# A recurrent-attention and mixer kernel on one core: plain up products in batches 1 and 2, casting loads for k of batch 0, and a new order of all steps

## Chip, core and metric

The kernel runs on one core of a Trainium2 chip. A core has TensorE (PE, the matmuls), VectorE (DVE), ScalarE (ACT), GpSimd (POOL) and SyncE (SP, which here only issues DMAs). POOL issues DMAs too, and only those can change the type of the data on their way. The metric is the device time of one launch in microseconds. Before the change the median of three runs is 233.54 us (233.43 to 233.62).

## What is computed

```python
B, H, S, D = 4, 8, 768, 64            # batches, heads, positions, head width; d_model = H*D = 512
state = gamma[h]*state + k_t v_t^T    # per batch and head, over the positions t
y_t   = q_t^T state / sqrt(D)
x     = y with the heads side by side                      # (4, 768, 512)
u     = x + ((x^T U) V)^T                                  # U 768x32, V 32x768
out   = u + relu(u @ w_ch1) @ w_ch2                        # 512x2048 and 2048x512
```

The inputs and the output are float32; the products run in bfloat16.

## The kernel before

The recurrence is computed in chunks: inside a chunk as masked scores, between chunks through a state of 64 by 64 per head. q, k and v are scaled by powers of gamma on the way, and the 1/sqrt(D) goes into q.

Every step of the kernel is one word of a list, `ORDER`. The word gives the step, its batch and block, the engine (E for PE, D for DVE, A for ACT, P for POOL, S for SP) and the PSUM banks that it opens. Each engine runs its steps in the order of the list, one behind the other, and waits at a step whose input is not there yet. The 8 banks of PSUM are handed out in the list as well: a step that opens a bank waits until the last reader of its former content is done. A second list, `LOADS`, gives the first loads in SP's queue.

The steps that matter here:

- **Head (batch 0).** `load_q6` (L274) and `load_early` (L284, L293) load q, k and v as float32. `ck` casts k to bf16 (`cast_early`, L440), `cv` scales v, `cq` scales q (L387), all in a layout with two neighbouring positions per partition. `tk`, `tq` turn k and q on PE (L458, L407), `ek`, `eq` copy the turned tiles from PSUM. `sc` are the scores (L474), `ma` the masking (L481), `st`, `cs` the states (L912) and their copies, `mx`, `qy`, `ox` the mixing (L502, L890, L902) and its copy into x. `pr`, `pc`, `xt`, `ex`, `uT` make u (L941 to L960). `fi` are filler matmuls on zeros (L932). `lu` and `lv` load U and, four times, V by casting loads from POOL (L346, L349).
- **Weights.** `w1a` to `w1e` and `w2.j` are casting loads from POOL (L352, L357). `gate` (L381) is a one-row copy on POOL that reads w2's third quarter and writes into the tile that q of batch 1 will use; so it holds POOL's queue until that quarter has landed, and the loads of q until then.
- **Attention of batches 1 to 3, in six chunks.** `lq`, `lk`, `lv` load a chunk (L376), `pk` casts k, `pq` and `pv` scale q and v (`prep`, L518). On ACT a scaling is eight instructions, one for each head (L527); on POOL or DVE it is one (L256). `dk`, `dq` turn k and q by a DMA transpose from SP (L554); batch 1 turns on PE. Then `sc` (L564), `ma` (L571), `st` (L582), `cs`, `mx` (L599, L604), `ox` as above.
- **u of batches 1 to 3.** `pj` (L623), `pc`, `xp` (L635), `xa` (L641) add the low-rank part; `du` turns x by DMA transposes (L647), in batch 1 PE does it (L654).
- **Up product, batch 0.** `U.b.m.h` (L721) is 4 matmuls of 384 columns into one bank: column block m of 16, half h of the positions. `V.b.m.h` is the relu that empties the bank (ACT L710, DVE L712).
- **Up product, batches 1 to 3.** Seven half-size products for each of 8 pairs of column blocks, `Q1` to `Q7` (L782), two matmuls each. They need sums of u (`us`, four on DVE) and of w1 (`VS`, 4 sets, once, written into w1's own tile). Behind them stand nine steps for each pair: copies `c1`, `c5`, `c6`, `c7`, adds `x2`, `x3`, `x7`, relus `r1`, `x4`, `r2`.
- **Down product, all batches.** Seven half-size products for each of 3 pairs of position blocks, `P1` to `P7` (L829), eight matmuls of 256 columns each, with sums of g before them (`s1` to `s4`) and of w2 (`Ta`, `Tb`, once), and adds (`c`, `a`, `x`) behind them. `s0`, `s1` with a `d` are the stores (L874).

Of the kernel before, what the change touches and what calls it, by code (L numbers as in the profile page):

```python
# [9 lines left out]
fp32 = mybir.dt.float32  # L10
# [5 lines left out]
LOADS = "q0 q1 q3 q2 k01 v01 k00 v00 k11 v10 v11 k10 k20 v20 v23 k21 v21 v22".split()  # L16
ORDER = (
# [175 lines left out]
def kernel(  # L193
# [72 lines left out]

    tmpA = big.tile([P, 12288], bf16, tag="gT", name="early_a")
    tmpB = big.tile([P, 9216], bf16, tag="sg", name="early_b")


    qin = {0: qin_tile(0)}

# [876 lines left out]
```

## Time and profile before

| what | value |
|---|---|
| median of 3 runs | 233.54 us (233.43 to 233.62) |
| the profiled execution, and its span | 231.99 us, 230.2 us |
| first up matmul, batch 0 | 28.25 us |
| first up matmul of batches 1, 2, 3 | 87.71, 139.03, 186.68 us |
| first down matmul of batches 0 to 3 | 53.27, 111.43, 163.29, 207.51 us |
| last matmul ends | 226.75 us |
| mean granted TensorE clock | 0.997 |
| chain that ended last | PE 43%, DVE 23%, ACT 11%, DMA 10% |

The page gives the busy time of each engine, the chain that is followed back from the last instruction, and groups of instructions by line and shape with their busy time, count and mean duration, and the idle time ahead of them. A helper's line stands for many steps: L249 is every ACT copy, L256 every two-input step on DVE or POOL, so the tiles and shapes tell the groups apart. Matmul records overlap, because the next one starts before the last one has left the array. DVE and ACT records overlap by a little as well, so that busy time over count is nearer to the distance between two starts than the mean duration is.

### The profile page before, as it was taken

The numbers are of one execution on the slowest core, as the hardware profiler recorded it, in microseconds if no ns is written. First come the engines' busy times: TensorE is split into PE (matmuls) and PEld (weight loads), VectorE is DVE, ScalarE is ACT, GpSimd is POOL, SyncE is SP. The second block draws the span as 40 slices with busy tenths as digits, with TensorE's granted clock in tenths as the row PEclk, the third lists the DMA queues.
The fourth block names the chain that finished last, engine by engine and source line by source line (L and its number), as shares of the span: only waits on it lengthen the run. The fifth ranks groups of instructions, "written<-read, shape, count | busy, mean of one in ns | idle before, by whom it ended". The sixth has DMA issues, their size and how long they took to land.

```text
span 230.2 us, 6231 instructions
## 1 busy us (share of the span) xinstructions
PE 210.3 (91%) x2420; PEld 149.8 (65%) x2420; DVE 190.4 (83%) x412; ACT 147.4 (64%) x400; POOL 97.5 (42%) x111
## 2 busy tenths in 40 slices
PE   7989999999699699997859999989999979999993
PEld 7977656557486576554546785545687856557883
DVE  5789488499978787999999767999899559999842
ACT  2578657678389998995994605888972127873100
POOL 3169125111999461585482224374371201442120
PEclk9999999999999999999999999999999999999998
DMA  6999999999989943895279479998732561001024
GB/s 191 307 289 173 162 173 256 235 197 231 209 175 231 216 77 67 168 230 138 54 145 171 104 149 175 212 236 101 152 114 71 137 117 46 3 0 48 0 111 165
DMA packets 86558, 34.73 MB, mean 151 GB/s; under 512 B 71233, under 2 KB 84161, under 8 KB 86529
## 3 DMA queue, kind: packets, MB, share of 16 engines
q1 hardware_dynamic: 79920, 27.01, 54.1%
q0 software_dynamic: 6608, 7.33, 16.6%
q8 instruction: 19, 0.31, 0.6%
q14 instruction: 11, 0.08, 0.1%
HBM read 27.75 MB, written 6.29 MB: 148 GB/s over the span
## 4 chain that ended last, share of the span: by engine, by line
PE 43%; DVE 23%; ACT 11%; DMA 10%; SPq 6%; issue 4%; DVEq 0%; POOL 0%
PE bank L782 17%; PE bank L829 16%; DVE gT L256 6%; DVE sg L256 5%; DMA qin<-in_q_dram 4%; ACT qd L527 3%; SPq L284 3%; DMA uT<-x 3%; ACT vd L527 3%; DVE gT L712 3%; DVE w2t L256 3%; DMA k<-in_k_dram 2%; PE bank L564 2%; DVE x L641 2%; SPq L647 2%
## 5 line engine op out<-in xcount | busy, mean ns | idle before, releaser
L249 ACT ACTIVATE part<-bank 128x384 f32<-128x384 f32 x73 | 33.6, 495 | 23.0 <-PE bank L782 22.3
L829 PEld LDWEIGHTS <-gT 128*128 128x128 bf16 x384 | 36.2, 98 | 5.7 <-issue 0.4
L256 DVE TENSOR_TENSOR gT<-bank,part 128x384 bf16<-128x384 f32 x64 | 32.5, 548 | 0.7 <-PE bank L782 0.5
L829 PEld LDWEIGHTS <-sg 128*128 128x128 bf16 x288 | 26.9, 98 | 9.3 <-issue 4.3
L710 ACT ACTIVATE gT<-bank 128x384 bf16<-128x384 f32 x50 | 23.8, 493 | 8.2 <-PE bank L721 7.6
L829 PE MATMUL bank<-w2b,sg 128*128 128x256 bf16 x192 | 24.6, 273 | 1.9 <-DVE a L571 1.9
L782 PEld LDWEIGHTS <-w1b 128*128 128x128 bf16 x192 | 17.9, 98 | 12.6 <-issue 1.5
L782 PE MATMUL bank<-uT,w1s 128*128 128x384 bf16 x96 | 21.6, 326 | 3.1 <-DVE part L251 1.4
L571 DVE TENSOR_TENSOR a<-bank,mask 128x512 bf16<-128x512 f32 x36 | 23.5, 681 | 1.1 <-PE bank L564 1.1
L829 PE MATMUL bank<-w2t,gT 128*128 128x256 bf16 x192 | 23.8, 273 | 0.2 <-ACT part_d L249 0.2
L829 PE MATMUL bank<-w2b,gT 128*128 128x256 bf16 x192 | 24.0, 273 | 0.0
L721 PE MATMUL bank<-uT,w1b 128*128 128x384 bf16 x128 | 22.3, 326 | 0.6 <-DVE gT L712 0.6
L782 PEld LDWEIGHTS <-w1s 128*128 128x128 bf16 x144 | 13.3, 98 | 14.1 <-issue 4.1
L527 ACT ACTIVATE vd<-in_v,gk 128x64 bf16<-128x64 f32 x88 | 22.0, 352 | 0.0
L782 PE MATMUL bank<-uS,w1b 128*128 128x384 bf16 x96 | 21.5, 326 | 0.3 <-DVE gT L256 0.2
L782 PE MATMUL bank<-uT,w1b 128*128 128x384 bf16 x96 | 21.3, 326 | 0.3 <-DVE gT L256 0.3
L641 DVE TENSOR_TENSOR x<-bank,x 128x256 bf16<-128x256 f32 x48 | 17.2, 416 | 3.5 <-PE bank L635 3.4
L256 DVE TENSOR_TENSOR o<-bank,part_d 128x256 f32<-128x256 f32 x34 | 14.2, 420 | 6.1 <-PE bank L829 5.8
L249 ACT ACTIVATE x<-bank 128x256 bf16<-128x256 f32 (+2 forms) x39 | 13.5, 387 | 6.7 <-PE bank L604 5.1
L721 PEld LDWEIGHTS <-w1b 128*128 128x128 bf16 x128 | 12.0, 98 | 8.5 <-issue 0.9
L256 POOL TENSOR_TENSOR sg<-sg,gT 128x768 bf16<-128x768 bf16 (+1 forms) x6 | 9.2, 1528 | 18.0 <-DVE sg L256 18.0
L256 POOL TENSOR_TENSOR gT<-part,part 128x384 bf16<-128x384 f32 x7 | 7.0, 1002 | 21.6 <-ACT part L249 21.6
(130 smaller groups left out, 407.2 us busy)
## 6 DMA issues: line engine op xcount, KB each, us to landing
in_k<-in_k_dram SPq DMA_DIRECT2D x18, 256.0 KB, 4.9
in_v<-in_v_dram SPq DMA_DIRECT2D x18, 256.0 KB, 5.0
out_dram<-o SPq DMA_DIRECT2D x13, 256.0 KB, 2.2
qin<-in_q_dram SPq DMA_DIRECT2D x8, 384.0 KB, 5.6
in_q<-in_q_dram SPq DMA_DIRECT2D x12, 256.0 KB, 4.1
out_dram<-o POOLq DMA_DIRECT2D x11, 256.0 KB, 2.7
w2b<-in_moe_w_ch_dram POOLq DMA_DIRECT2D x4, 512.0 KB, 12.7
k<-in_k_dram SPq DMA_DIRECT2D x6, 256.0 KB, 5.9
```

The source lines that it names most:

```text
L249: nc.scalar.activation(dst, src, AF.Copy)
L256: (nc.vector if eng == "D" else nc.gpsimd).tensor_tensor(dst, a, b, op=op)
L284: nc.sync.dma_start(out=t, in_=src)
L527: nc.scalar.activation(t[:, h], src[:, h], AF.Copy, scale=g[:, ci, h:h + 1])
L564: nc.tensor.matmul(sb[i][:, ts(hp, P)], kqT[b, ci][r, 0, hp], qt[r, hp], start=True, stop=True)
L571: nc.vector.tensor_tensor(live["a", b, ci][:, i], score_p[b, "s", ci][i].rearrange("p (n m) -> p n m", n=NHP), mask[:, None, :].to_broadca ...
L641: nc.vector.tensor_tensor(xg, live["h", b, jp][c][:, :256].rearrange("p (j e) -> p j e", j=2), xg, op=ALU.add)
L710: nc.scalar.activation(dst, src, AF.Relu)
L712: nc.vector.tensor_relu(dst, src)
L721: nc.tensor.matmul(g_p[:, :HT], w1b[:, c, ts(m, P)], uTs[b][:, c, ds(HT * h, HT)], start=(c == 0), stop=(c == NCB - 1))
L782: nc.tensor.matmul(dst[:, :HT], lhs[:, c], rhs(c), start=(n in (1, 2, 5) and c == 0), stop=(n in (2, 3, 4) and c == 1), skip_group_check=True)
L829: nc.tensor.matmul(dst, lhs[:, i], rhs[:, i], start=(n in (1, 2, 5) and i == 0), stop=(n in (2, 3, 4) and i == NI - 1), skip_group_check=True)
```

## The change

- Batches 1 and 2 use the plain up product (`U`, `V`) in place of `Q1` to `Q7`, their posts and the sums of u. Batch 3 keeps the seven products. The sums of w1 move from the first third of the list to the end of batch 2's up product.
- k of batch 0 is loaded by six casting loads from POOL (`Lk`) straight into bf16; the six casts `ck` go. The layout is [head, position pair] now, so that `turn_k` turns one head at a time, 8 transposes in place of 4 for each `tk`.
- U and V are loaded once as float32 by SP, at the end of `LOADS`, and cast on chip: U on POOL (`cU`), V four times (`cV0` on POOL, `cV1` to `cV3` on ACT).
- `g0`, a copy of one row on POOL, waits for the first piece of v's last block, ahead of w1's first load.
- w1's columns are asked for in the order a, b, c, d, e, and w1e behind the gate; w2's third quarter goes out between w1c and w1d.
- The whole order is new, and with it the engines of many steps. The scalings of q and v leave ACT altogether.

Steps of the main part by engine, where their number changes much:

| steps | before | after |
|---|---|---|
| Q products, U products | 168, 32 | 56, 96 |
| relus V in batches 1 and 2 | none | ACT 46, DVE 18 |
| scalings pq and pv | ACT 16, POOL 14 | POOL 26, DVE 4 |
| sums of w1 (sets) | POOL 3, DVE 1 | POOL 2, DVE 2 |

```diff
-LOADS = "q0 q1 q3 q2 k01 v01 k00 v00 k11 v10 v11 k10 k20 v20 v23 k21 v21 v22".split()
+LOADS = "q1 q0 q2 q3 v01 v00 v20 v11 v10 v23 v22 v21 V U".split()
...
+    lowr = big.tile([P, 4 * S], fp32, tag="w2t", name="lowr")
+    Vf = lowr[:RK, :S]
+    Uf = lowr[:, ds(S, NCK * RK)].rearrange("p (j r) -> p j r", j=NCK)
...
-    def load_u():
-        nc.gpsimd.dma_start(out=Ub, in_=moe_U.rearrange("(j p) r -> p j r", p=P))
-
-    def load_v(c):
-        nc.gpsimd.dma_start(out=V4[ds(RK * c, RK)], in_=moe_V)
+    def cast_u(eng):
+        copy(eng, Ub, Uf)
+
+    def cast_v(c, eng):
+        copy(eng, V4[ds(RK * c, RK)], Vf)
...
-    kb = [carve(tmpA, 3072 * i, [2, H, D]) for i in range(NB)]
+    kb = [carve(tmpA, 3072 * i, [H, 2, D]) for i in range(NB)]
...
+    def load_k0(B0, f):
+        nc.gpsimd.dma_start(
+            out=kb[B0][:, ds(4 * f, 4)].rearrange("p h j d -> p h (j d)"),
+            in_=k[0, ds(4 * f, 4), ds(256 * B0, 256), :].rearrange(
+                "h (t j) d -> t h (j d)", j=2))
...
     def turn_k(B0, f):
         tps[B0, f] = bank(bf16)
-        for hp in (2 * f, 2 * f + 1):
+        for n in range(2):
             for j in range(2):
-                nc.tensor.transpose(tps[B0, f][:, ts(2 * (hp % 2) + j, P)],
-                                    kb[B0][:, j, ds(2 * hp, 2)], ident)
+                for i in range(2):
+                    nc.tensor.transpose(
+                        tps[B0, f][ds(D * i, D), ts(2 * n + j, P)],
+                        kb[B0][:, 4 * f + 2 * n + i, j], ident)
...
+        elif nm == "g0":
+            nc.gpsimd.tensor_copy(out=hold, in_=early["v", 2, 0][:1, 0, :8])
```

The new order in the places that the steps of the prediction touch, in its own words: POOL's part of the head, the start of batch 1's up product, and the place where batch 2's down product meets batch 3's up product.

```
Lk00:P cq0:P ... Lk01:P Lk21:P Lk20:P ... Lk11:P ... Lk10:P ... cv00:P ... g0:P ... cv20:P ... cv11:P ... w1a:P
... cv23:P cv22:P ... cv21:P ... cU:P ... w1b:P ... cV0:P ... w1c.0:P ... w2.2:P ... w1d.0:P ... gate.0:P ... w1e.0:P ... w2.3:P

pj.1:E:3 ... tu.1.1:E:3 xp.1.2:E:0627 ... st.2.0:E:4 ... P4.0.d2:E ... ou.1.1:A U.1.14.0:E:5 ... U.1.2.0:E:7 ... tu.1.2:E:6

P6.2.d2:E Q1.3.0:E:5 ... P4.2.d1:E ... Q5.3.0:E:1 ... P7.2.d2:E ... P3.2.d1:E ... Q1.3.1:E:7 Q6.3.0:E Q1.3.2:E:4
Q5.3.1:E:2 ... P2.2.d2:E:6 ... P4.2.d2:E ... P3.2.d2:E Q2.3.0:E:6
```

More of the change, by code (lines that the diff above doesn't have):

```diff
@@ L280, in load_early @@
     def load_early(nm, B0, f):
-        src = {"k": k, "v": v}[nm][0, ds(4 * f, 4), ds(256 * B0, 256), :].rearrange(
+        src = v[0, ds(4 * f, 4), ds(256 * B0, 256), :].rearrange(
             "h (t j) d -> t h (j d)", j=2)
@@ L295 @@
     for nm in LOADS:
-        if nm[0] == "q":
+        if nm == "U":
+            nc.sync.dma_start(out=Uf, in_=moe_U.rearrange("(j p) r -> p j r", p=P))
+        elif nm == "V":
+            nc.sync.dma_start(out=Vf, in_=moe_V)
+        elif nm[0] == "q":
             load_q6(0, int(nm[1]))
@@ L311, in ramp @@
         return t
+    hold = consts.tile([1, 8], fp32)
     zeros = consts.tile([P, 512], bf16)
@@ L440, in cast_early @@
     def cast_early(nm, B0, f, eng, h0=0, nh=4):
-        dst = {"k": kb, "v": vb}[nm][B0]
         hs = ds(4 * f + h0, nh)
-        dst = dst[:, :, hs]
         src = early[nm, B0, f][:, ds(h0, nh)].rearrange("p h (j d) -> p j h d", j=2)
-        if nm == "k":
-            copy(eng, dst, src)
-        else:
-            scale = gk2[:, B0, hs].rearrange("p h j -> p j h")
-            binary(eng, dst, src, scale[:, :, :, None].to_broadcast([P, 2, nh, D]),
-                   ALU.mult)
+        scale = gk2[:, B0, hs].rearrange("p h j -> p j h")
+        binary(eng, vb[B0][:, :, hs], src,
+               scale[:, :, :, None].to_broadcast([P, 2, nh, D]), ALU.mult)
+    def load_k0(B0, f):
[3 more added lines that the diff above has]
+                "h (t j) d -> t h (j d)", j=2))
     tps = {}
@@ L912, in state0 @@
                     nc.tensor.matmul(st_p[ds(D * i, D), ds(P * c + D * i, D)],
-                                     kb[B0][r, j, 2 * c + i], vb[B0][r, j, 2 * c + i],
+                                     kb[B0][r, 2 * c + i, j], vb[B0][r, j, 2 * c + i],
                                      start=False, stop=True, skip_group_check=True)
@@ L970, in early_step @@
             turn_q6_out(0, x[0], eng)
-        elif k2 == "ck":
-            cast_early("k", x[0], x[1], eng)
+        elif k2 == "Lk":
+            load_k0(x[0], x[1])
         elif k2 == "tk":
@@ L1013, in early_step @@
             out_uT(x[0], 0, eng)
-        elif nm == "lu":
-            load_u()
-        elif nm == "lv":
-            for c in range(NCB):
-                load_v(c)
+        elif nm == "cU":
+            cast_u(eng)
+        elif k2 == "cV":
+            cast_v(x[0], eng)
+        elif nm == "g0":
+            nc.gpsimd.tensor_copy(out=hold, in_=early["v", 2, 0][:1, 0, :8])
         elif nm in ("w1a", "w1b"):
```

329 rows, old and new, of the table ORDER are left out of this document.

## The prediction

> **What bounds the kernel now.** I read the page's busy rows first, then the stages in a table of windows, then the groups, then the chain. I cut the span at the first matmul of each up product (U) and down product (D) of batches 0 to 3. The columns are: stretch, length, then PE, PEld, DVE, ACT and POOL busy, clock, DMA share, GB/s.
>
> ```profile
> PE 210.3 (91%) x2420; PEld 149.8 (65%) x2420; DVE 190.4 (83%) x412; ACT 147.4 (64%) x400; POOL 97.5 (42%) x111
> ```
> ```profile
> 0.00:28.25 28.25, 26.37 (x516) 21.96 (x517) 19.93 (x46) 17.18 (x41) 12.87 (x26) 1.00 1.05 225
> 28.25:53.27 25.02, 23.87 (x184) 14.03 (x181) 19.88 (x44) 16.62 (x33) 7.00 (x8) 1.00 1.14 218
> 53.27:87.71 34.44, 30.01 (x439) 23.68 (x437) 28.44 (x66) 29.51 (x99) 24.95 (x22) 1.00 0.87 183
> 87.71:111.43 23.72, 22.31 (x194) 12.36 (x192) 23.09 (x45) 20.20 (x46) 12.21 (x13) 1.00 0.66 142
> 111.43:139.03 27.60, 24.24 (x315) 19.14 (x313) 23.09 (x47) 15.54 (x59) 10.46 (x11) 1.00 0.66 129
> 139.03:163.29 24.26, 22.39 (x194) 12.53 (x192) 23.14 (x47) 20.47 (x52) 11.70 (x11) 1.00 1.00 190
> 163.29:186.68 23.39, 23.39 (x315) 19.07 (x313) 18.65 (x44) 9.92 (x33) 8.48 (x11) 1.00 0.48 104
> 186.68:207.51 20.83, 19.00 (x114) 10.85 (x112) 19.69 (x42) 15.40 (x34) 6.21 (x5) 1.00 0.10 38
> 207.51:226.75 19.24, 18.68 (x170) 16.18 (x167) 14.11 (x36) 2.51 (x7) 3.65 (x5) 1.00 0.19 70
> ```
>
> The stages are the head, then U0, D0, U1, D1, U2, D2, U3, D3. In the three seven-product stages (U1, U2, U3) DVE is busy 94 to 97% of the time; in D0 ACT is busy for 29.5 of 34.4 us. PE seems as full, but its records overlap. The groups say 326 ns for a 384-column matmul, while the chain has 32 of them in a row in 5.20 us:
>
> ```profile
> 77.73 1.91 ACT qd L527 x8
> 79.80 1.91 ACT qd L527 x8
> ...
> 82.50 1.91 ACT qd L527 x8
> ...
> 97.59 5.20 PE bank L782 x32
> ```
>
> So one costs 0.163 us from start to start. In the PE timeline 24 down matmuls of 256 columns take 2.78 us, 0.109 each. Counting all PE steps of a stage at such pitches (score 0.33, state 0.245, mixing 0.48, projection 0.45, expansion 0.31 us a step) gives PE's bare work: 23.3, 28.0, 21.0, 22.8, 20.9, 22.8, 18.3, 18.3 us, together 175.4. The stages took 198.5. The difference, 23.1 us (1.7, 6.4, 2.7, 4.8, 3.4, 0.6, 2.5, 0.9), is PE waiting. Most of it lies in D0, D1 and U2. The chain runs through it on DVE and ACT, as the three scalings above show: eight small ACT instructions each, 1.91 us.
>
> The Trainium skill ("Perfetto Trace Analysis", Identifying the Most-Contended Engine) says that matmul busy time does not measure how full PE is, as matmuls are pipelined. The rows agree (326 against 163 ns). By busy time the added matmuls would cost 32 x 0.326 = 10.4 us; nothing below uses that.
>
> **Up product of batches 1 and 2.** Seven products on 8 blocks are 112 matmuls; sixteen columns by two halves by four steps are 128. PE gains 2 x 16 x 0.163 = 5.2 us. Around it much goes:
>
> ```profile
> L249 ACT ACTIVATE part<-bank 128x384 f32<-128x384 f32 x73 | 33.6, 495 | 23.0 <-PE bank L782 22.3
> L256 DVE TENSOR_TENSOR gT<-bank,part 128x384 bf16<-128x384 f32 x64 | 32.5, 548 | 0.7 <-PE bank L782 0.5
> L710 ACT ACTIVATE gT<-bank 128x384 bf16<-128x384 f32 x50 | 23.8, 493 | 8.2 <-PE bank L721 7.6
> L527 ACT ACTIVATE vd<-in_v,gk 128x64 bf16<-128x64 f32 x88 | 22.0, 352 | 0.0
> ```
>
> Busy over count: an ACT copy 0.46, a DVE add 0.51, an ACT relu 0.476. Batch 1 has 36 DVE steps of this kind (x2, x3, c7, relus, four sums of u), 18.6 us; the new order has 11 relus of 0.53, 5.9 us. On ACT 40 steps, 20.7 us, become 21, 10.0 us. Batch 2: DVE 17.8 to 3.7, ACT 20.4 to 11.9. The sums of u go with them; PE waited 0.32 us for one in batch 2 (at 141.74). With fewer posts, banks are freed sooner.
>
> **Scalings and casts.** V and q scalings on ACT (8 x 0.25 = 2.0 us) fall from 16 to none; POOL gets 12 more at 1.03 to 1.11, DVE 4 at 0.69. POOL gives back 9 sums of g, two sets of w1 sums (4.6 each, now late) and six adds. Main part, before and after, by rows: ACT 143 to 95 us, DVE 184 to 164, POOL 87 to 77. What is late next is PE itself.
>
> **The order.** Stage by stage PE's bare work becomes 22.5, 28.6, 25.6, 21.2, 26.5, 14.5, 23.5, 18.3 = 180.7; DVE's 21.4, 28.5, 22.3, 16.5, 21.0, 16.5, 23.2, 14.2. Six or seven down products of batch 2 now stand between the first products of batch 3, so they cover the transposes (DMA, 4.0 us in the chain at 183.5) and part of the last DVE-heavy stage. In U0 two sets of sums stand ahead of q's cast, where DVE idled 3.98 us for the load. Against it: in D0 DVE and PE have equal work (28.5 and 28.6), and DVE does all w2 sums before the first products can go on.
>
> I let each stage be the larger of the two engines plus a rest: U0 24.0, D0 31.0 (about 2.5 us of rest against 4.0 over DVE's sum now), U1 26.6, D1 23.2, U2 28.0, D2 15.5, U3 25.0, D3 19.2, together 192.5. The rest is 11.8 us against 23.1, chosen half because two of three busy engines are relieved and the third is not. Bounds: 6 (all waits for posts and scalings go) and 23.1 (none do).
>
> **The head.** Out: six casts (ACT 4 x 0.63, POOL 0.61, DVE 0.67), four SP issues net, POOL's five U and V loads (3.0). In: six casting loads on POOL. POOL's rows for issuing run from 0.52 (V) to 1.01 (U); a quarter of w1 has as many runs as a k load, so 0.80, 4.8 in all; POOL waited 8.4 us there. U's cast and V's four (POOL about 0.6, ACT 0.8 by its 128x768 row) lie beside PE's fillers, and so do 24 more transposes (1.3 us of PE; 118 fillers of 128 columns become 114).
>
> POOL waits now: the cast of q0 (landed by 4.95, 1.73 long) holds back five k loads until about 6.7 to 10; the small copy on v20 holds back w1a; U's cast holds back w1b, and the first U step reads w1b's columns. U is SP's last load; the 14th issue ended near 14 before, plus 4.9 to land, so w1b goes at about 19, as before (19.4). The gate holds w1e until w2's first part lands. Issued near 20 and on its way 10.3 us as before (22.25 to 32.6), that is 30; with 8.8 to 12.5 to land w1e is due at 39 to 43, and the 23rd U step wants it at 42: up to 1 us.
>
> The last k then lands near 16 instead of 18.7. But 4.7 MB must come in at the 307 GB/s of the page's best slice: not before 15.4 plus landing. Gain at most 2.4. If a casting load lands like a part of w2 (12.7 median), the last k comes at 22.7, a loss of 2.8. I take a gain of 1.0, nearest to the k row (5.9 to landing).
>
> The Trainium skill ("DMA: Bandwidth & Descriptors", Specifications) speaks against this part: below 512 B a transfer leaves line rate through read-modify-write, and the casting loads write 256 B runs. Here in_k loads with 256 B runs land in 4.9 us, k's with 512 B in 5.9, so no trace bears it out for plain loads; none shows a casting one.
>
> **Sum.** First U at 27.25, + 192.5 = 219.75, + 3.45 from the last matmul to the end = span 223.2. The profiled execution took 231.99 for a span of 230.2, so 225.0. The median of the runs shown, 233.54, is 1.0067 of it: **226.5 us**.
>
> **Rivals.**
>
> *PE's price is not repaid (slower).* The waits are latencies between single steps, so 23.1 stay and 5.3 of work come on top, less 1.0 in the head: 234.5 span, 236.3 with its margin, 237.9 by the ratio. Place: U1 and U2. It decides from the point where the rest shrinks by less than 4.3. For it: U3, with DVE at 94%, still lost only 2.5 us. Against: ACT's scalings and DVE's adds stand in the chain in long pieces. 12%.
>
> *POOL blocks DVE.* A sum on DVE alone takes 0.55, beside a POOL sum 1.81:
>
> ```profile
> 198.74 0.55 DVE L256 TENSOR_TENSOR sg<-sg,gT 128x768 bf16<-128x768 bf16 x1
> 199.39 1.81 DVE L256 TENSOR_TENSOR sg<-gT,sg 128x768 bf16<-128x768 bf16 x1
> ```
>
> Twelve more scalings on POOL at 1.25 each are 15 us of DVE; if half falls on the path, 234.0, no change. Against: POOL loses 17 sums of the same kind. 4%. The Trainium skill ("SBUF — State Buffer", on the shared port pair) gives the rule: DVE with two SBUF inputs and a POOL instruction that reads SBUF exclude each other for a whole instruction. The row agrees.
>
> *Part of the gain goes* to a late head (+3.8) or to such blocking, or to pieces that wait for POOL's scalings in D0: 229 to 233. 13%.
>
> *Waits go almost wholly:* rest 6 instead of 11.8: 220.7. 15%.
>
> The forecast, 222 to 229, has 56%. Faster by over 0.2% (what a measurement of this kernel can tell): 56 + 13 + 15 = 84%; same 4%; slower 12%. Range 219.5 to 236: it reaches past the full relief and into the slower case.
>
> **What would show it.** Right: ACT under 105 us, DVE near 170; U1 and U2 at 26 to 29 with DVE under 90%; D0 no longer on ACT; D2 near 16; first U at 26 to 28. Wrong: D0 still at 34 with PE waiting for POOL's scalings; DVE sums of 1.8 in number; first U at 30; U1 and U2 near 30 with the same rest as now.

## The result, and the profile after

The changed kernel takes 241.66 us, median of 4 runs (240.50 to 242.98), beside 233.49 for the kernel before (231.15 to 233.62): ratio 1.0376, 95% interval 1.0291 to 1.0461. It is slower by 8.2 us, where 226.5 was forecast. The profiled execution took 242.98 us for a span of 241.2, the longest of the four and the one with the lowest mean clock (0.927; the others have 0.940 to 0.948). Some executions of most kernels here, the one before among them, are over 3 us longer than the fastest, most of them at a lower mean clock; the ratios leave them out.

The page of the changed kernel, busy row and the row of the granted clock (40 slices of 6 us, in tenths):

```profile
PE 225.0 (93%) x2472; PEld 160.2 (66%) x2472; DVE 172.4 (71%) x369; ACT 107.2 (44%) x236; POOL 93.2 (39%) x114
...
PEclk9975555999997999999999999999999979999999
```

ACT and DVE lost work as forecast (147 to 107, 190 to 172 us). But PE's busy time rose by 15 us, and the clock row, which held only nines and at its end an eight before, falls to 5 in the head and to 7 twice behind it. The stages cut as in the prediction (stretch, length, then PE, PEld, DVE, ACT, POOL busy, clock, DMA share, GB/s):

```profile
0.00:40.51 40.51, 34.70 (x536) 27.29 (x537) 19.38 (x47) 17.05 (x34) 20.95 (x37) 0.68 1.06 201
...
63.71:99.88 36.17, 31.69 (x455) 25.19 (x453) 30.12 (x63) 15.37 (x32) 17.12 (x18) 0.95 0.50 109
99.88:126.42 26.54, 26.54 (x267) 15.95 (x265) 20.67 (x40) 15.88 (x36) 9.33 (x10) 1.00 0.81 138
...
148.36:176.71 28.35, 27.89 (x283) 16.28 (x280) 19.29 (x39) 15.53 (x37) 7.41 (x8) 1.00 0.71 149
...
191.35:218.84 27.49, 25.54 (x162) 16.22 (x160) 22.55 (x44) 16.39 (x35) 12.62 (x11) 0.94 0.11 39
```

| | head | U0 | D0 | U1 | D1 | U2 | D2 | U3 | D3 | tail | span |
|---|---|---|---|---|---|---|---|---|---|---|---|
| before | 28.25 | 25.0 | 34.4 | 23.7 | 27.6 | 24.3 | 23.4 | 20.8 | 19.2 | 3.45 | 230.2 |
| forecast | 27.25 | 24.0 | 31.0 | 26.6 | 23.2 | 28.0 | 15.5 | 25.0 | 19.2 | 3.45 | 223.2 |
| after | 40.51 | 23.2 | 36.2 | 26.5 | 21.9 | 28.4 | 14.6 | 27.5 | 18.9 | 3.5 | 241.2 |

The span is 18.0 us over the forecast: 13.26 in the head, 4.7 behind it (5.2 in D0 and 2.5 in U3, less 3.0 in the rest). Against the kernel before, the head lost 12.26 and everything behind it gained 1.3. The new up products did what was said: U1 and U2 stand within 0.4 us of the forecast.

D0 and U3 hold a stretch of 3.4 us at half clock each (granted clock 0.50, from 72.9 and from 195.8; their mean clock above is 0.95 and 0.94). So a part of their 5.2 and 2.5 us is the clock: at full clock, with the old head (experiment 1), they took 34.9 and 26.7 us, which is 3.9 and 1.7 over the forecast.

What PE waits for (in all, times, longest), the longest rows:

```profile
PE bank L828 <- DVE w2b L243: 4.5, 2, 3.2
PE bank L456 <- DMA early_a<-in_k_dram: 3.6, 3, 2.3
PE bank L781 <- DVE uT L243: 1.9, 1, 1.9
```

The second is the head: transposes of k waiting for casting loads. The first stands in D0, the third at the start of U3. The chain in the head (start, length, what) names the same loads:

```profile
5.28 1.47 POOL early_b L243
6.75 1.50 POOL early_a L444 x2
8.25 9.92 DMA early_a<-in_k_dram
```

POOL first casts q0, then issues k, and the piece that decides takes 9.9 us to land. But 3.6 us of waits do not make 12 of loss. The larger part is the clock; in shorter windows:

```profile
12.00:14.00 2.00, 2.00 (x31) 1.63 (x29) 1.99 (x2) 0.81 (x1) 2.00 (x4) 0.50 1.71 185
...
15.00:18.00 3.00, 1.91 (x57) 1.39 (x55) 1.12 (x3) 1.19 (x2) 1.83 (x4) 1.00 1.42 225
...
20.00:30.00 10.00, 10.00 (x191) 7.96 (x192) 6.08 (x11) 4.61 (x8) 4.07 (x6) 0.50 0.89 124
30.00:40.00 10.00, 9.23 (x119) 6.64 (x116) 3.45 (x11) 5.74 (x17) 3.15 (x5) 0.50 1.12 242
...
42.00:44.00 2.00, 2.00 (x25) 0.97 (x25) 1.45 (x5) 1.25 (x3) 0.00 (x0) 0.96 1.21 196
```

After the longest wait for k (2.27 us, from 8.8 to 11.1) the clock is 0.50 from 11.4 to 14.8. After waits of 0.33 and 0.97 us for k (at 16 to 18 us) it is 0.50 from 18.3 on, and it stays there until 42.2, behind the first up matmul. PE looks completely busy in that time because each matmul takes longer: 32 mixing matmuls 1.67 us, where the kernel before needed 1.00. A busy share alone would have hidden this; the clock column beside it shows it.

### The profile page after: what moved, and what is told of

Its sections match the earlier page's. It is cut to its first block, busy times and chain, and to the rows that moved or that the text cites. A ratio compares the mean times of both kernels' runs of the same rounds, so it can differ in the third digit from the quotient of the medians.

```text
span 241.2 us, 6080 instructions
## 1 busy us (share of the span) xinstructions
PE 225.0 (93%) x2472; PEld 160.2 (66%) x2472; DVE 172.4 (71%) x369; ACT 107.2 (44%) x236; POOL 93.2 (39%) x114
## 4 chain that ended last, share of the span: by engine, by line
PE 71%; DMA 12%; SPq 6%; DVE 6%; POOL 2%; issue 1%; ACT 1%; DVEq 0%; POOLq 0%
PE bank L828 25%; PE bank L720 20%; PE bank L781 8%; DMA early_a<-in_k_dram 4%; SPq L646 4%; DMA in_q<-in_q_dram 2%; PE bank L603 2%; PE bank L563 2%; DMA uT<-x 2%; DMA qin<-in_q_dram 2%; DVE sg L243 1%; DVE w2t L243 1%; PE bank L501 1%; DMA in_v<-in_v_dram 1%; PE bank L901 1%
## 5 line engine op out<-in xcount | busy, mean ns | idle before, releaser
L720 PE MATMUL bank<-uT,w1b 128*128 128x384 bf16 x384 | 67.7, 328 | 0.0
L720 PEld LDWEIGHTS <-w1b 128*128 128x128 bf16 x384 | 35.9, 98 | 23.6 <-issue 0.8
L709 ACT ACTIVATE gT<-bank 128x384 bf16<-128x384 f32 x82 | 39.2, 492 | 27.6 <-PE bank L720 26.6
L828 PEld LDWEIGHTS <-sg 128*128 128x128 bf16 x288 | 27.9, 101 | 10.5 <-DVE w2b L243 3.4
L570 DVE TENSOR_TENSOR a<-bank,mask 128x512 bf16<-128x512 f32 x36 | 23.4, 685 | 7.1 <-PE bank L563 6.9
L243 POOL TENSOR_TENSOR vd<-in_v,gk 128x512 bf16<-128x512 f32 x17 | 17.8, 1055 | 12.3 <-DMA in_v<-in_v_dram 9.8
L711 DVE TENSOR_SCALAR gT<-bank 128x384 bf16<-128x384 f32 x22 | 12.1, 556 | 8.4 <-PE bank L720 5.7
L236 ACT ACTIVATE ns<-bank 128x256 bf16<-128x256 f32 (+2 forms) x20 | 8.3, 416 | 19.2 <-PE bank L581 12.4
L243 POOL TENSOR_TENSOR part_d<-part_d,x 128x256 f32<-128x256 f32 x10 | 6.9, 688 | 25.4 <-ACT part_d L236 25.2
L236 ACT ACTIVATE part<-bank 128x384 f32<-128x384 f32 x23 | 10.7, 489 | 10.6 <-PE bank L781 4.5
L828 PE MATMUL bank<-w2t,sg 128*128 128x256 bf16 x96 | 13.3, 288 | 0.0
L931 PE MATMUL bank<-zeros 128*128 128x128 bf16 x115 | 11.4, 266 | 1.2 <-DVE zeros L310 1.2
L243 POOL TENSOR_TENSOR qd<-in_q,gq 128x512 bf16<-128x512 f32 x9 | 9.3, 1042 | 5.9 <-DMA in_q<-in_q_dram 5.9
```

The costliest lines, as they stand in the source:

```text
L236: nc.scalar.activation(dst, src, AF.Copy)
L243: (nc.vector if eng == "D" else nc.gpsimd).tensor_tensor(dst, a, b, op=op)
L570: nc.vector.tensor_tensor(live["a", b, ci][:, i], score_p[b, "s", ci][i].rearrange("p (n m) -> p n m", n=NHP), mask[:, None, :].to_broadca ...
L709: nc.scalar.activation(dst, src, AF.Relu)
L711: nc.vector.tensor_relu(dst, src)
L720: nc.tensor.matmul(g_p[:, :HT], w1b[:, c, ts(m, P)], uTs[b][:, c, ds(HT * h, HT)], start=(c == 0), stop=(c == NCB - 1))
```

## The experiments

Eleven kernels, one of them run twice. "First U" is the first up matmul, the end of the head.

**1. The old head with the new main part.** The order of the kernel before up to its first up step, then the new order from its own first up step on.

```
-f0:E:0 cq1:D z0:E:1 ... ov.2:D eu.3:E U.0.3.0:E:6 ov.1:A xp.0.1:E:1523
+cq0:D cq1:D late.0:D ... eu.2:E ov.2:D U.0.3.0:E:6 xp.0.1:E:1523
```

> The head of the kernel before (k and v by plain loads and casts, U and V by casting loads, the fillers as they were) and then the new main part with its order; the fourth quarter but one of w1 comes before the last. Nothing of the computation is left out. Theory A (the head carries the loss, and the low clock and the late start of batch 0's down stage follow from it): first up matmul at 28.3 as before, D0 near 31 instead of 36.2, granted clock 0.99, span 223 to 226, ratio about 0.97. Theory B (the new main part is itself no faster): the stages stay as in the changed kernel's trace, 200.7 from the first up matmul to the end, span 229, ratio 0.995. Theory C (PE's price is not repaid): 234 and more.

Measured: first U 28.75, clock 1.00, span 229.6; ratio 0.9959 (0.9914 to 1.0005). Theory B: the head carries the loss against the kernel before, but the main part is no faster either, 200.85 us from the first U to the end against 202.0 before and 200.7 after (the last with the half clock in D0 and U3). D0 took 34.9, U2 29.5, U3 26.7. So two steps of the prediction failed, not one.

**2. More fillers in the changed kernel**, 40 ahead of the first k, 8 and 18 ahead of the next waits:

```
-fi3:E tq2:E:4 tk00:E:5
+fi3:E tq2:E:4 fi9:E fi9:E fi9:E fi9:E fi4:E tk00:E:5
```

> The changed kernel with 66 more filler matmuls on zeros in the head: 40 ahead of the first transposes of k, where PE stood idle for 2.27 us, 8 and 18 ahead of the next two waits for k. Nothing is left out. Theory A (PE's idle stretch brings the low granted clock, and the clock costs most of the 12.3 us): granted clock near 1.0 from 15 to 40 us, first up matmul at 31 to 34, span 232 to 235. Theory B (the data are late, the clock only follows): the fillers take the place of waits, first up matmul at 39 to 41, span 239 to 241.

Measured: first U 34.76, span 234.9, ratio 1.0106 (1.0036 to 1.0177). The clock was 1.00 up to 30.9 us; then a wait of 0.92 us at 29.2 (for a copy on ACT) was followed by half clock from 30.9 to 37.7. Useless work that fills waits takes 5.8 us off the head: theory A, but for this second fall of the clock.

**3. The remaining gap filled too**, 16 more fillers ahead of that wait:

```
-pr42:E pr52:E
+pr42:E fi9:E fi7:E pr52:E
```

> The kernel with 66 more fillers, and 16 fillers more ahead of the projection steps for which PE waited 0.92 us at 29.2, after which the clock fell to half from 30.9 to 37.6. Nothing is left out. Theory A (a short gap of PE in the stage of small matmuls brings the clock down, 6.7 us at half cost 2 before the first up matmul and 1.4 after it): clock 1.0 throughout the head, first up matmul at 32.5 to 33.5, span 231 to 232.5. Theory B (the drop at 30.9 comes from the whole stretch since 20, not from that gap): clock falls near 31 all the same, first up matmul at 34.8, span 235.

Measured: first U 33.24, span 233.2; executions of 235.0 and 235.7, too few for an interval. The head at full clock throughout:

```profile
10.00:20.00 10.00, 10.00 (x246) 8.65 (x244) 5.95 (x10) 3.84 (x6) 6.19 (x9) 1.00 1.32 204
20.00:30.00 10.00, 9.93 (x258) 7.75 (x253) 8.27 (x20) 6.84 (x17) 4.26 (x7) 1.00 0.83 103
```

The fillers do not make a load land earlier, they take the place of the waits. So the 40.51 - 33.24 = 7.3 us of the head's loss are mainly the clock; these are two single executions, and the first is the longest of its kernel. 5.0 us are left that are not the clock (33.24 against 28.25).

**4. The kernel before without its 48 fillers** between the first q and k transposes.

> The kernel before without the 48 filler matmuls that stand between the first q transposes and the first k transposes; nothing of the computation is left out, and no load or cast moves. Theory A (an idle stretch of PE of 2 to 3 us brings the clock down for tens of us): granted clock well under 1.0 between 10 and 40 us, first up matmul later by 3 to 10 us, ratio 1.015 to 1.045. Theory B (idle time of PE costs nothing while data are late): clock 1.0, first up matmul at 28.3, ratio 1.00.

Measured: ratio 0.9947 (0.9896 to 0.9997). Neither theory as stated. In the profiled execution (235.2 us, beside a fastest of 230.3) the clock did fall, from 10.5 to 13.9, after waits of 1.08 and 0.56 us, but first U was 28.57: 3.4 us at half clock cost 0.3 there. Beside the changed kernel, where 23.9 us at half clock ran past the first up matmul, this says that what such a fall costs depends on how long it lasts and on the work that it meets.

**5. and 6. One part alone: k by casting loads**, in the order of the kernel before, run twice, since the first profiled execution took 402 us and its times are of no use.

```
-cq0:D cq1:D late.0:D cq3:D z0:E:0
+Lk01:P Lk00:P Lk11:P Lk10:P Lk20:P Lk21:P cq0:D cq1:D late.0:D cq3:D z0:E:0
...
-cq2:D ck01:A fi6:E
+cq2:D fi6:E
```

> The kernel before, its order and its loads, with k of batch 0 alone changed: six casting loads at the head of POOL's queue, in the order of the kernel before (block 0, 1, 2), k's new layout and its eight transposes a piece; no casts of k. Nothing is left out. Theory A (casting loads are late by themselves, landing 8 to 10 us after a serial issue): the last k transposes come after 21 us, first up matmul at 30 to 33, ratio 1.01 to 1.02. Theory B (what was late is block 1's k, which the new order asks for last): the k transposes come as before, the last near 19.4, first up matmul at 27 to 29, ratio 0.99 to 1.00.

> The kernel before with k of batch 0 alone by casting loads, once more, since the profiled execution of the first time took 402 us and shows no usable times. Nothing is left out. Its timed runs (235.6 and 237.7) speak for casting loads that are late by themselves: first up matmul at 30 to 32, v's pieces landing 8 to 12 us after issue instead of 5 to 7. If U and V carry the loss of the run with both (first up matmul at 32.3): first up matmul here at 28 to 29.5.

Measured: ratio 1.0111 (0.9993 to 1.0228), then 1.0180 (1.0116 to 1.0244); first U 30.52 at full clock, the last k transposes at 21.53 instead of 19.38. Casting loads lose 2.3 us by themselves, even when all six are issued from 2.5 us on. The last k transposes before, and with k cast:

```profile
19.38 0.40 PE L458 MATMUL bank<-ident,early_a 128*128 128x128 bf16 x4
```

```profile
21.53 0.41 PE L453 MATMUL bank<-ident,early_a 128*64 128x128 bf16 x8
```

The loads up to 24 us, before and then with k cast (KB each, median us from issue to landing; ahead of them POOL's queue with its packets, MB and share of 16 engines):

```profile
k<-in_k_dram SPq DMA_DIRECT2D x6, 256.0 KB, 5.9
v<-in_v_dram SPq DMA_DIRECT2D x4, 256.0 KB, 6.6
```

```profile
q0 software_dynamic: 4284, 1.10, 47.6%
v<-in_v_dram SPq DMA_DIRECT2D x4, 256.0 KB, 11.5
early_a<-in_k_dram POOLq DMA_DIRECT2D x6, 128.0 KB, 11.3
```

k needs 11.3 instead of 5.9 us, and v, which was not touched, 11.5 instead of 6.6. Part of this is earlier issue: k was issued from 2.5 to 7.1 us instead of 2.8 to 14.4, and v moved up in SP's queue. The delay in itself is smaller, 2.2 us for the last k transposes and 1.5 for POOL's first scaling of v (12.36 instead of 10.86). On one queue the pieces came one after the other in the order in which PE wants them; on two queues all are on their way at once and all come late. Nor does the halved output show as saved transfer time: in the first 24 us POOL's queue (k, then U, V and some of w1) moved 4284 packets in 47.6% of 16 engines, 42.7 ns for 257 bytes written, and SP's 41.6 ns a packet of 640 bytes. (The two queues' shares, 47.6 and 57.7%, sum to more than one, so these times can hold waits of one queue for the other.) The Trainium skill ("DMA: Bandwidth & Descriptors", SWDGE vs HWDGE vs iDMA) says that the two kinds of queue feed different queues within each DMA engine and are served in turn; the landing times agree with it. Its rule (Specifications) that transfers below 512 B leave line rate, which I had set aside for want of a casting row, agrees in direction: as much time for less than half the bytes; a read-modify-write as such no run shows.

**7. Both loads changed, old order kept**: the same, and U, V by SP's last loads with casts on chip.

> The kernel before with the head's loads all changed but its order kept: k by casting loads as in the run before this one, U and V as SP's last two loads and cast on chip (U on POOL just ahead of w1's second quarter, V on ACT and POOL). Nothing is left out. Theory A (loads are at fault): first up matmul at 31 or later, ratio over 1.01. Theory B (the order of the new head is at fault): first up matmul at 27.5 to 29.5, ratio within 0.6% of one; against the run before this one at most 0.5 us, by U's cast holding w1.

Measured: first U 32.33, 1.8 later than with k alone. One execution took 235.0, no interval; the profiled one (241.0) lost clock only behind the head. This 235.0 lies under the five executions in the ratios of experiments 5 and 6 (235.6 to 237.7), so the 1.8 us are shown by the two traces and not by the times. U's cast, at 22.65, held w1's next quarter until 22.94, where the kernel before issued it at 19.42. From here to the gap-filled kernel with the new order (33.24) the order adds 0.9. Theory A: the loads are at fault, the order hardly.

**8. The changed kernel with k by plain loads again**, six casts on ACT and DVE put just ahead of the transposes.

```
-LOADS = "q1 q0 q2 q3 v01 v00 v20 v11 v10 v23 v22 v21 V U".split()
+LOADS = "q1 q0 q2 q3 k00 v01 k01 v00 k21 k20 v20 k11 v11 k10 v10 v23 v22 v21 V U".split()
```

> The changed kernel with k of batch 0 alone undone: six plain loads of k on SP's queue again, in the new list of loads, and six casts (five on ACT, one on DVE) just ahead of the transposes; k's new layout, the casts of U and V and the order stay. Nothing is left out. If the casting loads of k are what is late: no wait of PE over 1 us for k, clock near 1.0, first up matmul at 28 to 31, span 226 to 231. If U, V or the order of the head are at fault as well: first up matmul at 34 to 40.

Measured: first U 34.99, ratio 1.0256 (1.0169 to 1.0343). It does not separate what it should: PE now waited 1.2, 1.4 and 0.5 us for the late casts, and the clock fell twice (from 11.7 to 15.2 and from 32.2 to 39.1). Experiments 5 to 7 answered the question instead.

**9. and 10. What brings the clock back?** 40 fillers in one block ahead of the last k transposes, and 54 in nine groups from the fifth transposes on.

```
-st2:E ma201:D cs2:A cv21:P tk10:E:5
+st2:E ma201:D cs2:A cv21:P fi9:E fi9:E fi9:E fi9:E fi4:E tk10:E:5
```

> The changed kernel with 40 more fillers (full 128x128 matmuls on zeros) in one block ahead of the last transposes of k, within the stretch of 23.6 us at half clock. Nothing is left out. Theory A (the head's matmuls of 64x64 tiles and transposes cannot bring the clock back, full ones can; it came back 1.6 us after the first up matmul): the granted clock goes back to 1.0 within 3 to 7 us of the block's start and stays there, the block costs 4.3 us at half pitch and saves up to 6, first up matmul at 38 to 41. Theory B (the clock comes back after a fixed time, whatever PE does): half clock until 42, first up matmul at 44 to 45.

> The changed kernel with 54 more fillers (full 128x128 matmuls on zeros) in nine groups of six, spread over the stretch of the head that ran at half clock (from the fifth transposes of k to the last mixing steps); PE's waits ahead of it stay. Nothing is left out. Theory A (in a stage of 64x64 tiles the clock, once down, needs full matmuls to come back): half clock for one or two pieces of 3.4 us only, mean clock of all executions 0.96 or more against 0.927 to 0.948 in the changed kernel, first up matmul at 36 to 39. Theory B (it comes back by its own count or by the up stage alone): half clock from 18 to beyond 42 as before, mean clock 0.92 to 0.95, first up matmul at 44 to 46 (54 fillers at half pitch are 5.8 us).

Measured: with the block half clock from 16.8 to 23.6, and again from 33.8 to 40.7, around a wait of 1.19 us for a copy on ACT; first U 38.94, ratio 1.0299 (1.0242 to 1.0355); but the clock was back 0.4 us before the block began, so this run says nothing of what the block does. With the groups half clock from 16.3 to 26.6, back while they ran (from 22.2 on); mean clock of the executions 0.951 to 0.965 against 0.927 to 0.948; first U 40.52, as in the changed kernel, and 243.1 us, ratio 1.0458 (1.0392 to 1.0523). So the fillers paid in time about what they saved. Theory A is likelier than B (nothing lasted to 42), but its times came out too low, and the first run shows a return without the block. What ends a stretch at half clock is not settled.

**11. Two scalings of v from POOL to ACT**, in the kernel of experiment 1. Its trace shows what PE waits for in D0. DVE and POOL there, then PE (in brackets the idle time before, and what ended it):

```profile
53.31 1.68 DVE L235 TENSOR_TENSOR sg<-sg,gT 128x384 bf16<-128x384 bf16 x1
...
55.75 1.15 DVE L235 TENSOR_TENSOR w2t<-w2b,w2t 128x512 bf16<-128x512 bf16 x1
56.82 1.26 DVE L235 TENSOR_TENSOR w2t<-w2b 128x512 bf16<-128x512 bf16 x1
```

```profile
53.09 1.69 POOL L235 TENSOR_TENSOR sg<-gT,sg 128x768 bf16<-128x768 bf16 x1 [3.29 <-DVE sg L235]
55.45 2.35 POOL L235 TENSOR_TENSOR vd<-in_v,gk 128x512 bf16<-128x512 f32 x2 [0.68 <-DMA in_v<-in_v_dram]
```

```profile
53.53 0.81 PE L808 MATMUL bank<-w2b,gT 128*128 128x256 bf16 x6 [1.50 <-DMA w2b<-in_moe_w_ch_dram]
...
58.89 0.39 PE L808 MATMUL bank<-w2b,sg 128*128 128x256 bf16 x2 [1.59 <-DVE w2b L235]
60.59 0.81 PE L808 MATMUL bank<-w2b,sg 128*128 128x256 bf16 x6 [1.32 <-DVE w2b L235]
```

Each long DVE sum lies beside a POOL instruction and ends within 0.3 us of it; without a neighbour such sums take 0.36 and 0.42. With a fourth (0.72 beside a cast of k) the excess is 1.32 + 0.73 + 0.84 + 0.30 = 3.19 us. PE waits 2.91 for these sums, and 1.50 before them for w2's landing.

```
-pv.1.1:P pv.1.0:P
+pv.1.1:A pv.1.0:A
```

> The kernel with the old head and the new main part, in which two of batch 1's scalings of v (chunks 0 and 1) go from POOL to ACT, which idles 6.1 us there. Nothing is left out. In that kernel's trace PE waits 1.59 and 1.32 us for DVE's sums of w2 in D0; the sums of w2 that run beside those scalings take 1.15 and 1.26 us instead of 0.42. Theory A (POOL's scalings hold DVE's sums, and the sums hold PE): these sums fall back to 0.42, PE's wait for sums of w2 falls from 2.9 to about 1.3, D0 from 34.9 to 33.2 or 33.5, span 227.5 to 228.5. Theory B (the landing of w2's last part at 53.5 and the number of sums set it): PE's wait stays at 2.5 to 2.9, D0 34.5 to 35, span 229 to 230.

Measured: ratio 0.9875 (0.9827 to 0.9922), executions of 228.8 to 231.2, where the kernel without this edit had 231.4 to 233.1. The profiled execution (239.5) lost clock in the head (first U 36.40) and cannot give D0's length. The same sums there, and PE's waits:

```profile
63.68 0.42 DVE L235 TENSOR_TENSOR w2t<-w2b,w2t 128x512 bf16<-128x512 bf16 x1
64.03 0.42 DVE L235 TENSOR_TENSOR w2t<-w2b 128x512 bf16<-128x512 bf16 x1
```

```profile
64.96 0.39 PE L808 MATMUL bank<-w2b,sg 128*128 128x256 bf16 x2 [1.59 <-DVE w2b L235]
...
66.67 0.81 PE L808 MATMUL bank<-w2b,sg 128*128 128x256 bf16 x6 [1.31 <-DVE w2b L235]
```

The sums are back at 0.42, as theory A says. PE's wait for sums of w2 is not: it is 2.90 as before, which is what theory B says. But this execution has no wait for w2's landing, so PE comes to the sums 1.5 us earlier. The waits together fall from 4.41 to 2.90 us, and the first of these products starts 5.67 instead of 7.25 us after D0 began. In the changed kernel, which had no wait for landing either, the wait for the sums was 4.5. So theory A, by the times and by the sums' rows; its figure for the wait did not come true. The 1.68 beside POOL's sum of g is still there.

**12. POOL's other neighbours moved as well**: two sums of g to DVE, the sums of w2 in the order in which the products want them, two sets of w1 sums from D2 into U2.

```
-Tb.3:D Ta.0:D P1.0.d0:E:2 Tb.0:D eq.1.2:A eq.1.0:A Ta.1:D Tb.1:D
+Ta.0:D P1.0.d0:E:2 eq.1.2:A eq.1.0:A Ta.1:D Tb.3:D Tb.0:D Tb.1:D
...
-s4.0.6:P s3.0.7:D c5.0.d0:D ek.1.0:A cq.1.1:D s4.0.4:P P6.0.d0:E
+s3.0.7:D s4.0.4:D s4.0.6:D c5.0.d0:D ek.1.0:A cq.1.1:D P6.0.d0:E
...
-V.2.13.0:A st.3.4:E
+V.2.13.0:A VS.6:P st.3.4:E
...
-s4.2.7:P V.2.1.1:A
+s4.2.7:P VS.0:P V.2.1.1:A
...
-xa.3.1.1:D VS.0:P xa.3.1.2:D
+xa.3.1.1:D xa.3.1.2:D
...
-c1.3.1:A VS.6:P x2.2.d2:D
+c1.3.1:A x2.2.d2:D
```

> The run before this one, and besides: two fourth sums of g of batch 0 go from POOL to DVE and behind the sums of w2; the sums of w2 that the fifth product needs come ahead of those that the sixth needs; two sets of w1 sums on POOL (0 and 6) move from the middle of D2 into U2, so that they do not stand beside DVE's sums of u at the start of U3, where PE waited 1.9 us. Nothing is left out. If POOL's neighbours of DVE are what both stages lose to: D0 32 to 33, first wait of U3 under 1 us, span 225.5 to 227, ratio 0.975 to 0.985. If what PE waits for is DVE's own count of sums and u's transposes: D0 33.5 or more, U3's wait as it was, span 228 to 229.5.

Measured: 225.36 us (224.86 to 226.38), span 223.8, ratio 0.9703 (0.9651 to 0.9755): faster than both kernels. The same sums of g and w2, and the stages D0 and U3:

```profile
52.86 0.36 DVE L235 TENSOR_TENSOR sg<-sg,gT 128x384 bf16<-128x384 bf16 x1
...
55.57 0.42 DVE L235 TENSOR_TENSOR w2t<-w2b,w2t 128x512 bf16<-128x512 bf16 x1
```

```profile
51.74:84.01 32.27, 30.16 (x454) 24.44 (x452) 26.87 (x64) 18.67 (x47) 13.11 (x15) 1.00 0.93 189
...
177.18:201.16 23.98, 23.87 (x163) 15.56 (x160) 19.90 (x44) 16.39 (x35) 7.40 (x7) 1.00 0.12 45
```

D0 falls from 34.9 to 32.3 and U3 from 26.7 to 24.0, as expected; PE no longer waits for sums of w2 or of u. The span came out 1.7 us under what was expected. The run changes three things at once, POOL's sums of g, the order of the sums of w2 and the place of the w1 sums, and does not say what each is worth. From the first U to the end it takes 194.95 us; the forecast had 195.95. The Trainium skill ("SBUF — State Buffer", on the shared port pair) says that DVE with two SBUF inputs and a POOL instruction that reads SBUF exclude each other for a whole instruction. The rows agree: 0.36 alone, 1.68 beside a POOL sum of 1.69.

## Why the prediction was wrong

**What bounds the kernel: right.** DVE and ACT held the seven-product stages, and with the plain product in batches 1 and 2 they no longer do: DVE is busy for 20.7 of 26.5 us in U1 and for 19.3 of 28.4 in U2.

**Up product: right.** U1 26.5 for 26.6, U2 28.4 for 28.0, D1 21.9 for 23.2, D2 14.6 for 15.5. PE's price was repaid there, so the rival that put the slower case into U1 and U2 had the sign and not the place.

**The head: the step that failed.** It says "I take a gain of 1.0, nearest to the k row (5.9 to landing)". Measured by the experiments in a row of single executions, the head went from 28.25 by k's casting loads to 30.52 (+2.3), by U and V to 32.33 (+1.8), by the order to 33.24 (+0.9), and by the waits and the clock to 40.51 (+7.3). Two things failed in it:
- Landing. I took a row of the same size on another queue and let each load land alone. The casting loads took 8.1 to 10.3 us in the changed kernel, and v became later with them (8.8 for 6.6). The bound of the loss, 2.8, was not far off for k alone (2.3), though its own landings (22.7 against 18.7) are 4.0 apart and it does not say why it counts 2.8 of them; U and V came on top, which I had put beside the fillers.
- The clock. The page had a clock row of nines, and I took it for granted. The fillers were counted (118 to 114), but not asked what they keep up: a wait that they do not cover can cost its length and then half of PE's speed. That is the largest single term, 7.3 us in the profiled execution, and it stands nowhere in the sum, the range or the rivals. The rival with a late head (+3.8) had the direction: without the clock's part the head came at 33.24, 6.0 us after the forecast.

What was said of POOL was right: issues of 0.75 to 0.91 us (0.80 forecast), five of them held behind q0's cast to 6.7 to 10.5 (forecast 6.7 to 10), w1's quarter at 20.5 (forecast 19), and no loss at the gate: U0 took 23.2.

**The order: half wrong.** "I let each stage be the larger of the two engines plus a rest." For D0 that gave 31.0, and it took 36.2 (34.9 with the old head). DVE has 28.5 and PE 28.6 us of work in D0, but not at the same time: DVE's sums come first and PE waits for them. The paragraph before says so, and the sum then allows 2.5 us for it; with the old head, at full clock, it was 34.9 - 28.6 = 6.3. The prediction's rest was 11.8 us. The changed kernel's stages leave 197.2 - 180.7 = 16.5, the half clock in D0 and U3 included, the last experiment's 191.5 - 180.7 = 10.8.

**POOL blocks DVE: the mechanism that I gave 4%.** I weighed it by count (12 more scalings, 17 fewer sums) over the whole kernel. The totals by rows were too large besides: the stages before add up to 170.1 us of DVE by the prediction's own windows, not 184, and after the change DVE took less than forecast in every stage (152.6 for 163.6 in all) but D0 (30.1 for 28.5). What counts is where POOL's instructions stand: four of them beside DVE's burst at D0's start, and a set of w1 sums beside the sums of u at U3's start. There, in the changed kernel, DVE's second sum of u and its third took

```profile
193.17 1.39 DVE L243 TENSOR_TENSOR uT<-uT 128x768 bf16<-128x768 bf16 x1
...
195.77 1.50 DVE L243 TENSOR_TENSOR uS<-uT 128x768 bf16<-128x768 bf16 x1
```

instead of 0.56, beside POOL's four sums of w1 (191.50 to 196.86), and PE waited 1.95 us. Moving these neighbours, with the reordered sums, was worth 229.6 - 223.8 = 5.8 us of span between two executions at full clock, about all that the main part lacked: 5.35 in D0 and U3, 1.02 in U2 and 1.08 from D3's first matmul to the end, less 1.55 in D2 and 0.10 in the head.

So the time of 226.5 was wrong because of the head, its clock above all, and of POOL's places. The gain that was argued for the rest of the change exists (225.4 in the last experiment), but in a kernel with the old head and with POOL's steps moved; that this is near 226.5 is partly chance, as the forecast counted a gain in the head and none from such moves.

## What to carry to other kernels

Read the clock row before pricing a wait of TensorE: where fillers cover the waits ahead of a stage, a load that comes 1 or 2 us later than they last can cost several times its delay. Price a load that moves to another queue together with those that it now overtakes, by what all of them land at when they are on their way together. And price work that moves to POOL by what DVE does at that very moment, not by the totals of a stage.

## What the runs showed of the hardware

- Half clock followed gaps of PE that were quite short: 0.92 us in experiment 2 (at 29.2), 0.91 us in experiment 8 (at 29.4), 2.27 us in the changed kernel (8.8 to 11.1). Gaps of 1.5 to 1.6 us in the heads of experiments 1 and 7 had no such effect; in the execution of experiment 11, which has the same head as experiment 1, one of 1.5 us had. The stretches at half, worked out from the clock in windows of 1 us, lasted 3.4 us (changed kernel, 11.4 to 14.8; experiments 4 and 8), 6.8 (experiments 2, 8 and 9), 10.2 (10), 20.5 (11) and 23.9 (changed kernel): 1, 2, 3, 6 and 7 times 3.41. The Trainium skill ("TensorE: Matmul & The Clock Gate", Part 1) describes a free-running window of 3.4 us, half clock after an idle window and full clock after a busy one. The lengths agree, and so does the play of chance; that a window must be idle as a whole does not agree, with a gap of 0.92 us in PE's records.
- In the changed kernel the clock stayed at half for 23.9 us in which PE's records show one idle time, of 0.77 us, but matmuls of 64x64 tiles and transposes, and came back 1.6 us into the full matmuls of the up product. That small matmuls do not count as busy would explain it, and experiment 10 speaks for it. But in experiment 9 the clock came back at 23.6, before the added fillers, and in experiment 11 at 36.4, as the first up matmul began; so the full matmuls of the up product are not needed, and the cause stays open.
- Casting loads showed no saving on the DMA engines for writing half the bytes: with both queues busy, 42.7 ns for a packet of 257 bytes written, 41.6 for a plain one of 640.
